# Three moves in the schedule of a fused adaLN block: the loads of stored attention results, the next q tile, and block 0's second norm

## The chip, the cores and the metric

The kernel runs on one core of one Trainium2 chip. Times are device microseconds of one execution (us). The metric is the median time of one launch; the trace is one profiled execution of the same program.

## The reference, cut to what matters

All arrays are fp32; S = 2048 tokens, D = 448, 16 heads of 28, F = 1792. Six vectors of the condition `c` (`sa`, `ca`, `ga` and `sb`, `cb`, `gb`) shift, scale and gate an attention branch and an MLP branch.

```python
mod = (_silu(c) @ w_mod).reshape(c.shape[0], 6, 1, -1)
sa, ca, ga, sb, cb, gb = (mod[:, 0], mod[:, 1], mod[:, 2], mod[:, 3], mod[:, 4], mod[:, 5])
h = _layernorm(x, axis=-1) * (1 + ca) + sa
x = x + ga * _A_ref(h, A_wqkv, A_wo)           # softmax attention over 16 heads, then @ wo
h = _layernorm(x, axis=-1) * (1 + cb) + sb
x = x + gb * _B_ref(h, B_w1, B_b1, B_w2, B_b2) # layernorm, @ w1 + b1, gelu, @ w2 + b2
```

So the second half begins with two layer norms in a row: the block's own, and after scale and shift the one inside `_B_ref`.

## The kernel before, in words

Matrix products keep fp32 accuracy by splitting operands into a high part `hi` and a rest `lo`, and adding three products. Tokens go in four blocks of 512 (`NB`), each of four tiles of 128.

**Phase 1** (to about 176 us) makes q, k and v. q and k are stored in DRAM (`dscr`) and read back in the layout that attention needs.

**Attention** is a loop over 16 units `u` = 0 to 15. Unit `u` is a group of four heads `g = u // 4` and a block of queries `qt = u % 4`. A unit has 16 steps, one per tile of 128 keys (`kt`), so the steps are numbered 0 to 255 and unit `u` begins at step 16u. One step emits, in this order:

1. at a fixed `kt`, `load_q(u + 1)`: two 256 KB loads of the next unit's q tile (L653 within `load_parts`);
2. `tick_late`, which puts ready row maxima into the q tile (L509 on VectorE, four small DMAs L512), once that tile was asked for;
3. twelve score matmuls into a two-bank PSUM tile `s` (L1162), with matmuls for the maxima of later units between them (L466) that VectorE reduces (L471), and two exponentials on ScalarE (L1167);
4. eight matmuls of the step before into `o` (L1132, function `av`); after a unit's last one `end_unit` copies `o` to `o_sb` on ScalarE (L1101);
5. whatever the table `sched` holds for this step. `at(step, fn)` appends to it; entries of one step run in the order in which they were appended. Entries made before the loop (norm, weights) thus stand ahead of those that `end_unit` makes within it.

Each engine runs its instructions in the order of emission, and so does SyncE's queue (SP), which issues nearly every DMA. An instruction that waits holds up all behind it on its engine.

**The end of a unit** is a chain of tasks counted from step `base + 1` with `base = 16(u + 1)`: `t_den` (the softmax sums go out by DMA, L880), `t_rec` (VectorE reciprocal L886, DMA to DRAM `drec` L888, broadcast back as `rb` L890), `t_split` (GpSimd multiplies `o_sb` by `rb`, L895) and `t_split2` (VectorE makes `hi`, L905; GpSimd makes `lo`, L906). Units 0 to 10 are "staged": they store hi and lo in DRAM (`doh`, L910). Units 11 to 14 finish a query block instead: `load_o` fetches the stored hi and lo of the earlier head groups into slots `a2h`, `a3h` and `b1h` (L868; four loads of 256 KB for unit 11, six for units 12 to 14), and the four tasks `t_wo(t)` at steps `base + 8` to `base + 11` multiply by `wo` (L386, nine to twelve matmuls into one PSUM tile), copy the result on ScalarE (L926) and add it to the residual `acc` on GpSimd (L927). Unit 15 needs no loads.

**PSUM tiles for small products** come from a ring, `ps_mx()`. During most of attention the ring has three banks. When no maxima are left, `third_tile(True)` gives two of them to a third score tile, and the ring is the single bank `m1`:

```python
    s_ring[:] = s_ring + ["s2"] if on else ["s1", "s0"]
    mx_ring[:] = ["m1"] if on else ["m1", "m2", "m2"]
```

**The second norm of block 0** (`ln2_stages(0)`) runs beside units 14 and 15. It has 14 numbered stages, one per step: the first statistics (stages 0 to 3, VectorE, L190 and L191; then GpSimd's power, L197), `mid` (4 to 7: VectorE normalises, L207; GpSimd multiplies and adds, L962 and L963), second statistics (6 to 9), `fin` (11 and 12: L207 and a copy, L968) and `addb` (10 to 13, GpSimd, L971). After them come four tasks `chunk(k)`, one per step: four transposes on TensorE (L267) into one `ps_mx()` tile, ScalarE's copy of it to `hi` (L994) and VectorE's subtraction for `lo` (L996, L998), both of which read that tile:

```python
            p = ps_o() if b and k == 3 else ps_mx()
            transposes(p, ys, k)
            hi = yT[b][0](k)
            act.copy(hi, p)
```

**Weights of the MLP** are fetched and split by `w_prep`: first loads at step 242 (L1014, L1016, L1017 and, for w2, L1035), then one item per step at steps 245 to 248 and 250 to 255 (VectorE, L1026 and L1027, or L1045 to L1048).

After step 255 comes the MLP (L1208 to L1237), which needs block 0's transposed norm at once.

The functions that the change touches, and their callers:

Of the kernel before, what the change touches and what calls it, by code (L numbers as in the profile page):

```python
# [27 lines left out]
NB = S // 512  # L28
NG = H // 4
NKT = S // 128  # L30
# [9 lines left out]
def tile_adaln_block(ctx: ExitStack, tc: tile.TileContext, x, wqkv, wo, w1, b1, w2, b2, c, w_mod, out):  # L40
# [29 lines left out]
    def nm(t):  # L70
        uid[0] += 1
        return f"{t}_{uid[0]}"

    def sbt(tag, shape, dt=F32, bufs=1):
        return sb.tile(shape, dt, tag=tag, name=nm(tag), bufs=bufs)

    def slot(tag, shape, dt=F32R):
        return sb.tile(shape, dt, tag="slot_" + tag, name=nm("slot_" + tag), bufs=1)
# [19 lines left out]
    def ps_mx():  # L98
        mx_ring.append(mx_ring.pop(0))
        return ps_tile(mx_ring[-1], 1 if mx_ring[-1] == "m1" else 2)  # L100

    def ps_o():
        return ps_tile("o")
# [4 lines left out]
    def f(t):  # L108
        return t.bitcast(F32)
# [254 lines left out]
    def put_spare(most=8):  # L364
        for kind, g, sl in spare[:most]:
            n = 4 * (4 * kind + g)
            for part in range(2):
                sp.dma_start(
                    by_head(f(dscr[1][part][3]))[:, n : n + 4, sl], by_head(f(dscr[kind][part][g]))[:, DH:32, sl],
                )  # L370
        del spare[:most]
# [10 lines left out]
    def mm_acc(p, terms, mid=None):  # L382
        for i, (a, b) in enumerate(terms):
            if mid and i == len(terms) // 2:
                mid()
            pe.matmul(p, a, b, start=(i == 0), stop=(i == len(terms) - 1))  # L386
# [223 lines left out]
    def finish_max(g, qt):  # L610
        while left[(g, qt)] > 0:
            emit_max(1)
# [35 lines left out]
    qst = {}  # L648
# [11 lines left out]
    def load_q(u):  # L660
        g, qt = divmod(u, NB)
        qst[u] = load_parts(f"b{u % 2}", 0, g, slice(qt * 512, (qt + 1) * 512))
# [33 lines left out]
    for b in range(NB):  # L696
        more = b + 1 < NB
        tasks = []
# [10 lines left out]
        for n, (tb, kind, g) in enumerate(tasks):  # L709
# [9 lines left out]
            k = n - (6, 4, 4, 4)[b]  # L719
# [17 lines left out]
            if more:  # L737
                k = n - (6, 4, 4, 4)[b]
# [122 lines left out]
    def last_g(qt):  # L861
        return NG - 2 if qt == NB - 1 else NG - 1

    def load_o(qt):
        for g, tag in zip(range(last_g(qt)), ("a2h", "a3h", "b1h")):
            t = slot(tag, [128, 2, 512])
            for part in range(2):
                sp.dma_start(f(t)[:, part, :], f(doh[part][g])[:, qt * 512 : (qt + 1) * 512])  # L868
            o_in[(qt, g)] = t

    def unit_end_tasks(u, o_sb):
        g, qt = divmod(u, NB)
        st = {}
        staged = g < last_g(qt)
        parts = [g] if g > last_g(qt) else list(range(g + 1))

        def t_den():
            q_ = pool if u == NU - 1 else sp
            den = sbt("den", [128, 16], bufs=2)
            q_.dma_start(den, o_sb[DH:128:32, :].rearrange("j (q r) -> j q r", r=16))  # L880
            st["den"] = den

        def t_rec():
            q_ = pool if u == NU - 1 else sp
            rec = st["den"]
            dve.reciprocal(rec, rec)  # L886
            drec = dr.tile([4, 512], F32, tag="drec", name=nm("drec"), bufs=2)
            q_.dma_start(drec.rearrange("j (q r) -> (j q) r", r=16), rec)  # L888
            rb = sbt("osb", [128, 512], bufs=2)
            q_.dma_start(rb, drec[:, None, :].broadcast_to([4, 32, 512]))  # L890
            st["rb"] = rb

        def t_split():
            st["on"] = st["rb"]
            pool.tensor_tensor(out=st["on"], in0=o_sb, in1=st["rb"], op=ALU.mult)  # L895

        def t_split2():
            on = st["on"]
            if u < NU - 1:
                hi = sbt("hi", [128, 512], F32R, bufs=3)  # L900
                lo = sbt("lo", [128, 512], F32R, bufs=3)
            else:
                hi = sb.tile([128, 512], F32R, tag=YTAGS[7], name="o_hi", bufs=1)
                lo = sbt("osb", [128, 512], F32R, bufs=2)
            dve.tensor_copy(hi, on)  # L905
            pool.tensor_tensor(out=lo, in0=on, in1=f(hi), op=ALU.subtract)  # L906
            st["hi"], st["lo"] = hi, lo
            if staged:
                for part in range(2):
                    sp.dma_start(f(doh[part][g])[:, qt * 512 : (qt + 1) * 512], f((hi, lo)[part]))  # L910

        def t_wo(t):
            def go():
                p = ps_mx()
                ts = slice(t * 128, (t + 1) * 128)
                terms = []
                for g_ in parts:
                    if g_ == g:
                        hi, lo = st["hi"][:, ts], st["lo"][:, ts]
                    else:  # L920
                        hi, lo = o_in[(qt, g_)][:, 0, ts], o_in[(qt, g_)][:, 1, ts]
                    w_hi, w_lo = wo_p[0][:, g_, :], wo_p[1][:, g_, :]
                    terms += [(hi, w_hi), (hi, w_lo), (lo, w_hi)]
                mm_acc(p[:, :D], terms)
                y = sbt("full", [128, 512], bufs=3)[:, :D]
                act.copy(y[:, :D], p[:, :D])  # L926
                pool.tensor_tensor(out=acc[qt][:, t, :], in0=acc[qt][:, t, :], in1=y[:, :D], op=ALU.add)  # L927

            return go


        times = (0, 4, 8, 9) if staged else (0, 1, 4, 5)
        tasks = list(zip(times, (t_den, t_rec, t_split, t_split2)))
        if len(parts) > 1 and not staged:
            tasks.append((0, lambda: load_o(qt)))
        if not staged:
            tasks += [(7 + t, t_wo(t)) for t in range(4)]
        return tasks
# [114 lines left out]
    NU = NG * NB  # L1053
    sched = {}

    def at(step, fn):
        sched.setdefault(step, []).append(fn)
# [10 lines left out]
    def b2_mul():  # L1068
        b2_row = sbt("row_b2g", [128, D])
        pool.tensor_tensor(out=b2_row, in0=rows["b2"][:, :D], in1=rows["gb"], op=ALU.mult)  # L1070
        rows["b2g"] = b2_row

    for i in range(5):
        at(1 + i, lambda: put_spare(1))
    for g in (1, 2):
# [3 lines left out]
    last0 = NKT * (NU - 1)  # L1079
    lnst = [ln2_stages(b) for b in range(NB)]  # L1080
    for i in range(14):
        at(last0 - 12 + i, lambda i=i: lnst[0][0](i))
    for k in range(NC):
        at(last0 + 3 + k, lambda k=k: lnst[0][1](k))
    q0, q1 = f"b{(NU - 2) % 2}", f"b{(NU - 1) % 2}"
    items = [w1_item(0, k, (q0, "a0")) for k in range(NC)]
    items += [w2_item(ft, ("v0", "a1")) for ft in range(0, 4)]
# [51 lines left out]
    for u in range(NU):  # L1139
        g, qt = divmod(u, NB)  # L1140
        for kt in range(NKT):
            step = u * NKT + kt
            if kt == 1 and u + 1 < NU and u + 1 not in qst:
                load_q(u + 1)
            if kt == NKT - 6 and u + 1 < NU:
                finish_max(*divmod(u + 1, NB))
            tick_late()
            if not (three or mxq or late):
                three = True
                third_tile(True)  # L1150
            pt = [slot(tags[step % len(tags)], [128, 2, 512], F32) for tags in ptags]
            n = n_maxima(step)
            n0 = 1 if n == 3 and step % 4 == 3 else 2

            ks, qs = kst[(g, kt // 4)], qst[u]
            kc = slice((kt % 4) * 128, (kt % 4 + 1) * 128)
            for hf in range(2):
                s2 = ps_s2()
                for term, (kp, qp) in enumerate(((0, 0), (1, 0), (0, 1))):
                    for jj in range(2):  # L1160
                        rows_ = slice(64 * hf + 32 * jj, 64 * hf + 32 * jj + DH + (term == 0))
                        pe.matmul(s2[:, jj, :], ks[rows_, kp, kc], qs[rows_, qp, :], start=(term == 0), stop=(term == 2))  # L1162
                    if hf == 0 and term < min(n0, n):
                        emit_max(1, 1)
                    if hf == 1 and term == 2 and n > n0:
                        emit_max(n - n0, 0)
                act.activation(pt[hf], s2, AF.Exp, scale=SCALE)  # L1167
            if step == 0:
                v_task(NB - 1, 3, ps_mx())
                emit_max(2)  # L1170
            if pend is not None:
                pu, pkt, pp, po = pend
                av(pu, pkt, pp, po)
                if pkt == NKT - 1:
                    end_unit(pu, po)
            if kt == 0:
                o = ps_o()
            pend = (u, kt, pt, o)
            if qt == NB - 1 and kt % 4 == 3 and g + 1 < NG:
                load_k(g + 1, kt // 4 if g else kt // 4 ^ 2)  # L1180
            for fn in sched.pop(step, ()):
                fn()
# [58 lines left out]
    for n in range(len(seq) + LAG):  # L1241
        if n < len(seq):
            b, i = seq[n]
# [53 lines left out]
```

## Time and profile before

| | |
|---|---|
| median of 3 runs | 1128.87 us (1128.83 to 1129.13) |
| the profiled execution's own time | 1130.08 us |
| its span (first to last instruction) | 1128.0 us |
| outside the span | 2.08 us |
| TensorE busy | 1116.4 us, 99% of the span |
| granted TensorE clock, mean | 1.00 |
| attention, by its `av` matmuls | 176.35 to 833.9 us |
| unit 13, 14, 15 from `t_den` to `t_den` | 692.2 to 742.0, to 789.6, to 834 us |

Reading it: PE is TensorE's matmuls, PEld its weight loads, DVE VectorE, ACT ScalarE, POOL GpSimd, SPq the DMA issues on SyncE's queue. In a timeline a row gives start and duration in us, engine, line of the kernel, operation, output and input tile, how many instructions were merged, and in square brackets how long the engine had been idle and what released it. In the chain of waits a row gives start, duration, and the work that nothing later could have started without. TensorE is pipelined, so busy TensorE is not TensorE at its peak, and a lost microsecond shows in the distance between equal steps better than in the busy share.

### The profile page before, as it was taken

Reading aid. Unit: us, or ns where it says so; the run is one execution under the profiler, and the core shown is the slowest. Engines: PE = TensorE matmul, PEld = TensorE weight load, DVE = VectorE, ACT = ScalarE, POOL = GpSimd, SP = SyncE. Lnnn points to the kernel's source line nnn. Section 1 sums busy time; section 2 is a strip of 40 time slices with the busy share of each in tenths; the row PEclk is TensorE's granted clock in tenths of the full one; section 3 lists DMA queues with packets and bytes.
Section 4 is the critical chain, followed back from the end, with each engine's and each line's share of the span. In section 5 each row is a group of like instructions: output and inputs, shape, how many; then the busy total and the mean of one; then the engine's idle time right before and its main releaser. Section 6 shows DMA issues by size and latency. Waiting matters only on the chain.

```text
span 1128.0 us, 20665 instructions
## 1 busy us (share of the span) xinstructions
PE 1116.4 (99%) x8319; PEld 670.1 (59%) x8319; DVE 843.7 (75%) x1485; ACT 672.0 (60%) x823; POOL 209.6 (19%) x211
## 2 busy tenths in 40 slices
PE   8999999999999999999999999999999999999998
PEld 6756674444444444444444454545468888888887
DVE  6968788999999999999999978595448853444322
ACT  4555657888887888788788867576752321111110
POOL 1533332110000000000000020217114504123000
PEclk9999999999999999999999999999999999999999
DMA  9562263121121211311111312020422100000000
GB/s 303 202 200 88 91 200 114 48 84 41 58 95 57 58 40 57 91 53 58 53 44 58 112 41 83 4 85 1 137 73 78 35 33 1 1 33 1 33 1 33
DMA packets 49341, 81.19 MB, mean 72 GB/s; under 512 B 12311, under 2 KB 18702, under 8 KB 49234
## 3 DMA queue, kind: packets, MB, share of 16 engines
q1 hardware_dynamic: 48762, 79.14, 22.1%
q8 instruction: 65, 1.06, 0.4%
q10 hardware_dynamic: 148, 0.46, 0.1%
q0 software_dynamic: 336, 0.28, 0.1%
q14 instruction: 30, 0.25, 0.1%
HBM read 55.04 MB, written 26.48 MB: 72 GB/s over the span
## 4 chain that ended last, share of the span: by engine, by line
PE 94%; DVE 3%; ACT 1%; DMA 1%; issue 1%; POOL 0%; SPq 0%; DVEq 0%; ACTq 0%; POOLq 0%
PE s L1162 26%; PE o L1132 22%; PE m L386 16%; PE pa L386 8%; PE m L466 6%; PE s L1232 3%; PE s L1233 3%; PE s L1231 3%; DVE mxp L471 2%; PE t L1232 1%; PE t L1233 1%; PE t L1231 1%; DMA slot_c<-in_w_mod_dram 1%; PE ma L466 1%; PE o L267 1%
## 5 line engine op out<-in xcount | busy, mean ns | idle before, releaser
L471 DVE TENSOR_REDUCE mxp<-m 128x1 f32<-128x512 f32 x884 | 568.8, 686 | 75.3 <-PE m L466 41.1
L1162 PE MATMUL s<-slot_b,slot_a 28*128 28x512 f32 (+1 forms) x3072 | 376.3, 420 | 0.0
L1162 PEld LDWEIGHTS s<-slot_b,slot_a 28*128 28x128 f32 (+1 forms) x3072 | 213.0, 184 | 247.4 <-ACT slot_c L1167 124.1
L466 PE MATMUL m<-kh,qh 28*128 28x512 f32 x863 | 287.6, 472 | 1.2 <-DVE mxp L471 0.9
L1167 ACT ACTIVATE slot_c<-s 128x1024 f32<-128x1024 f32 x170 | 174.3, 1025 | 75.9 <-PE s L1162 75.6
L1132 PE MATMUL o<-slot_c,v 128*32 128x512 f32 x680 | 178.8, 605 | 0.0
L1208 ACT ACTIVATE full<-m,b_col 128x512 f32<-128x512 f32 x56 | 38.6, 689 | 192.0 <-PE m L386 175.5
L1132 PE MATMUL o<-slot_c1h,v 128*32 128x512 f32 x512 | 134.7, 605 | 0.0
L1132 PE MATMUL o<-slot_c0h,v 128*32 128x512 f32 x512 | 134.7, 605 | 0.0
L1167 ACT ACTIVATE slot_c0h<-s 128x1024 f32<-128x1024 f32 x128 | 130.4, 1019 | 2.4 <-PE m L386 2.4
L1167 ACT ACTIVATE slot_c1h<-s 128x1024 f32<-128x1024 f32 x128 | 130.4, 1019 | 0.0
L1211 DVE CAST hi<-full 128x512 fp32r<-128x512 f32 x56 | 25.5, 455 | 134.6 <-ACT full L1208 134.6
L466 PEld LDWEIGHTS m<-kh,qh 28*128 28x128 f32 x863 | 114.3, 182 | 8.6 <-DVE mxp L471 5.1
L1167 ACT ACTIVATE slot_d<-s 128x1024 f32<-128x1024 f32 x86 | 88.1, 1025 | 39.3 <-PE s L1162 39.1
L895 POOL TENSOR_TENSOR osb<-osb,osb 128x512 f32<-128x512 f32 x16 | 20.9, 1307 | 441.1 <-DMA osb<-drec 356.8
L1132 PE MATMUL o<-slot_d,v 128*32 128x512 f32 x344 | 90.5, 605 | 0.4 <-ACT osb L1101 0.4
L386 PE MATMUL m<-y,slot_a 128*128 128x512 f32 x160 | 60.7, 395 | 0.0
L1132 PEld LDWEIGHTS o<-slot_c,v 128*32 128x32 f32 x680 | 24.5, 108 | 52.4 <-issue 49.5
L1212 DVE TENSOR_TENSOR lo<-full,hi 128x512 fp32r<-128x512 f32 x56 | 44.2, 788 | 5.9 <-DVE hi L1211 0.9
L471 DVE TENSOR_REDUCE mxp<-ma 128x1 f32<-128x512 f32 x54 | 35.6, 683 | 7.1 <-PE m L466 4.8
L386 PE MATMUL m<-y,slot_v 128*128 128x512 f32 x112 | 39.2, 396 | 0.0
L386 PE MATMUL m<-y,slot_b 128*128 128x512 f32 x112 | 39.0, 398 | 0.0
(316 smaller groups left out, 1626.7 us busy)
## 6 DMA issues: line engine op xcount, KB each, us to landing
slot_b<-d SPq DMA_DIRECT2D x32, 256.0 KB
slot_a<-d SPq DMA_DIRECT2D x32, 256.0 KB
d<-lo SPq DMA_DIRECT2D x28, 256.0 KB
d<-hi SPq DMA_DIRECT2D x16, 256.0 KB
osb<-drec SPq DMA_DIRECT2D x15, 256.0 KB
out_dram<-xn SPq DMA_DIRECT2D x16, 224.0 KB
raw<-in_B_w_dram SPq DMA_DIRECT2D x14, 224.0 KB
qh<-d SPq DMA_DIRECT2D x12, 256.0 KB
```

Of the source, the lines that this page charges most:

```text
L386: pe.matmul(p, a, b, start=(i == 0), stop=(i == len(terms) - 1))
L466: pe.matmul(m, qh_sb[(g, qt)][js, i * 128 : (i + 1) * 128], k[js, :], start=True, stop=True)
L471: dve.tensor_reduce(out=mxp[(g, qt)][:, i, j, cch : cch + 1], in_=m, op=ALU.max, axis=AX.X)
L1132: pe.matmul(o[32 * j : 32 * j + 32, :], v_sb[kt // 4][:, kt % 4, 4 * g + j, :], p[j // 2][:, j % 2, :], start=(kt == 0), stop=(kt == NKT - 1),
L1162: pe.matmul(s2[:, jj, :], ks[rows_, kp, kc], qs[rows_, qp, :], start=(term == 0), stop=(term == 2))
L1167: act.activation(pt[hf], s2, AF.Exp, scale=SCALE)
L1208: act.activation(gf, p, AF.Gelu_apprx_tanh, bias=b1_col[:, i : i + 1])
L1211: dve.tensor_copy(ghi, gf)
L1212: dve.tensor_tensor(out=glo, in0=gf, in1=f(ghi), op=ALU.subtract)
L1231: pe.matmul(pp, ghi[:, ts], w_hi, start=(m == 0), stop=False)
L1232: pe.matmul(pp, ghi[:, ts], w_lo, start=False, stop=False)
L1233: pe.matmul(pp, glo[:, ts], w_hi, start=False, stop=(m == NFT - 1))
```

## The change

Three things move; no instruction is added or removed.

- `load_o` for units 11 to 14 is no longer a task at `base + 1`, behind `t_den`. It stands in the table three steps before the end of the unit, at `base - 3`: steps 189, 205, 221 and 237.
- `load_q(u + 1)` is emitted at the unit's step 4 instead of its step 1.
- The second norm of block 0 is four steps later: its stages from steps 228 to 241 go to 232 to 245, its chunks from steps 243 to 246 go to 247 to 250.

```diff
         tasks = list(zip(times, (t_den, t_rec, t_split, t_split2)))
-        if len(parts) > 1 and not staged:
-            tasks.append((0, lambda: load_o(qt)))
         if not staged:
             tasks += [(7 + t, t_wo(t)) for t in range(4)]
...
+    for u in range(NU - NB - 1, NU - 1):
+        at(NKT * (u + 1) - 3, lambda qt=u % NB: load_o(qt))
...
     for i in range(14):
-        at(last0 - 12 + i, lambda i=i: lnst[0][0](i))
+        at(last0 - 8 + i, lambda i=i: lnst[0][0](i))
     for k in range(NC):
-        at(last0 + 3 + k, lambda k=k: lnst[0][1](k))
+        at(last0 + 7 + k, lambda k=k: lnst[0][1](k))
...
-            if kt == 1 and u + 1 < NU and u + 1 not in qst:
+            if kt == 4 and u + 1 < NU and u + 1 not in qst:
                 load_q(u + 1)
```

Here `last0` is 240, the first step of unit 15, `NKT` is 16, `NU` 16 and `NB` 4.

## The prediction

> **What bounds the kernel now.** I read the page first: busy time, then the chain of waits by engine.
>
> ```profile
> PE 1116.4 (99%) x8319; PEld 670.1 (59%) x8319; DVE 843.7 (75%) x1485; ACT 672.0 (60%) x823; POOL 209.6 (19%) x211
> PE 94%; DVE 3%; ACT 1%; DMA 1%; issue 1%; POOL 0%; SPq 0%; DVEq 0%; ACTq 0%; POOLq 0%
> ```
>
> TensorE carries 94% of the chain. An edit that moves other engines' work pays only where TensorE stands still for it. So I went through the chain of waits in order of time over units 13 to 15, where all three edits have their effects, and looked for steps longer than their like.
>
> ```profile
> 700.28 1.01 PE o L1132 x8
> ...
> 705.17 0.99 PE o L1132 x8
> ...
> 708.26 1.29 DVE mxp L471 x2
> ...
> 710.79 0.99 PE o L1132 x8
> ...
> 745.16 0.99 PE o L1132 x8
> ...
> 755.81 0.99 PE o L1132 x8
> ...
> 792.58 1.07 PE s L1162 x12
> ...
> 802.74 0.91 PE s L1162 x11
> ...
> 809.97 0.47 PE m L386
> 810.44 0.92 PE s L1162 x11
> ...
> 812.36 2.63 PE m L386 x12
> 814.99 0.91 PE s L1162 x12
> ...
> 824.07 0.91 PE s L1162 x12
> ...
> 829.96 1.07 PE s L1162 x12
> ```
>
> Three stalls show.
> - Unit 13: two steps with maxima take 4.89 us (700.28 to 705.17), the next two 5.62, with VectorE on the chain between. Lost: 0.73 us.
> - Unit 14, steps 228 to 231: four steps take 10.65 us (745.16 to 755.81) instead of 2 x 4.89. Lost: 0.87 us.
> - Unit 15: the score matmuls of steps 243, 247, 249, 250 and 252 begin at 792.58, 802.74, 810.44, 814.99 and 824.07. A plain step takes 1.96 us (824.07 to 829.96 is three), a step with a chunk 2.54 (four in 10.16), a `t_wo` step 4.55. Steps 247 and 248, one plain and one `t_wo`, take 7.70 instead of 6.51. Lost: 1.19 us, ahead of the last matmul of `t_wo(0)` at 809.97.
>
> Next, the timelines of VectorE, SP and GpSimd at these places tell why.
>
> ```profile
> 707.92 0.43 DVE L905 CAST hi<-osb 128x512 fp32r<-128x512 f32 x1 [1.12 <-POOL osb L895]
> ...
> 751.33 0.62 DVE L190 BATCH_NORM_STATS2 st<-acc 128x6 f32<-128x448 f32 x1
> 751.99 0.18 DVE L191 BATCH_NORM_AGGREGATE mv<-st 128x2 f32<-128x6 f32 x1
> ...
> 781.05 1.33 DVE L207 TENSOR_SCALAR xn<-xn,mv,rs 128x448 f32<-128x448 f32 x1 [2.13 <-POOL rs L197]
> ...
> 786.92 0.20 DVE L968 COPY xn<-xn 128x64 f32<-128x64 f32 x1
> 791.45 0.25 DVE L886 RECIPROCAL den<-den 128x16 f32<-128x16 f32 x1 [4.34 <-DMA den<-osb]
> ```
>
> ```profile
> 265.92 0.32 SPq L888 DMA_DIRECT2D drec<-den  x1
> 267.33 0.55 SPq L890 DMA_DIRECT2D osb<-drec  x1
> ...
> 737.58 0.80 SPq L653 DMA_DIRECT2D slot_b<-d  x2
> ...
> 768.65 2.28 SPq L512 DMA_DIRECT2D slot_b<-full  x4
> ...
> 790.25 0.89 SPq L868 DMA_DIRECT2D slot_a2h<-o  x2
> ...
> 793.30 0.90 SPq L1014 DMA_DIRECT2D raw<-in_B_w_dram  x2
> 794.30 0.50 SPq L888 DMA_DIRECT2D drec<-den  x1
> 800.32 0.56 SPq L890 DMA_DIRECT2D osb<-drec  x1
> ```
>
> ```profile
> 775.44 1.17 POOL L962 TENSOR_TENSOR xn<-xn,row_cb 128x448 f32<-128x448 f32 x1
> ...
> 778.90 1.14 POOL L927 TENSOR_TENSOR acc<-acc,full 128x448 f32<-128x448 f32 x1 [1.06 <-ACT full L926]
> 780.00 1.02 POOL L197 TENSOR_TENSOR rs<-ve,cst 128x4 f32<-128x4 f32 x1
> ...
> 806.71 1.28 POOL L895 TENSOR_TENSOR osb<-osb,osb 128x512 f32<-128x512 f32 x1 [20.95 <-ACT slot_c L1167]
> 808.60 1.32 POOL L906 TENSOR_TENSOR lo<-osb,hi 128x512 fp32r<-128x512 f32 x1 [0.60 <-DVE hi L905]
> ```
>
> In unit 13 VectorE stood 1.12 us at L905, waiting for the multiplication L895, with maxima queued behind. In unit 14 the first statistics (0.62 + 0.18 us, four times) sit between maxima that already fill VectorE. In unit 15 `lo` ends at 809.92, and TensorE goes on at 809.97. `lo` is late because `drec`, issued at 794.30 behind six loads of L868 and two weight loads, took until 800.32 to let `rb` go: 6.02 us, against 1.41 with nothing ahead (265.92 to 267.33). The page names an exponential as L895's releaser, but the row that fits is `rb`, issued 6.39 us before.
>
> **The change part by part.**
>
> **load_o, four steps earlier.** It leaves the queue between `den` and `drec`. At `base - 3` it waits for the last `t_wo` of the unit before, at `base - 5`. Behind it on SP stands only the next `den`, over 8 us later. Its data is wanted at `base + 8`. Price of the move: nothing. In unit 15 the two weight loads remain ahead of `drec`, now issued right behind `den`, and the reciprocal cannot come before 791.45. So `drec` goes at about 791.7, `rb` 1.41 to 6.02 us later. I take 2.5, near the quiet row, since a quarter of the load traffic is left: 794.2. With the old 6.39 us, L895 begins at 800.6 and `lo` is done near 804. At 6.02 it would be 807.5. `t_wo(0)` needs `lo` for its last product, after 809 in the new schedule (below), so even the upper end is covered. Gains: the 0.73 us of unit 13, where `rb` needs to be just over 1 us earlier, and the 1.19 us of unit 15. Each lies between 0 and its measured loss; I take all.
>
> **load_q, three steps later.** Before, it was issued well ahead of `den` (737.58 for unit 15). Now it comes behind `den`, and for units 11 to 13 behind `rb` too. The tile is written by the maxima DMAs only 31 us later (768.65) and read in the next unit. In staged units it also pushes L509 and the four maxima DMAs (2.28 us) from step 1 to step 4, ahead of `drec`. That costs `drec` at most these 2.28 us, while `t_split` is a fixed four steps (9.8 us) behind `t_rec` there. VectorE gets L509 beside the reciprocal, about half a microsecond together, less than one maximum. Cost: 0; if the cover were gone, the four maxima DMAs once per unit.
>
> **The second norm, stages.** The statistics go to steps 232 to 235. These are `t_wo` steps, in which almost no maxima are left, so VectorE is free. Gain: 0.87 us, bounds 0 and 0.87. The price is lateness. GpSimd's `mid` pairs (L962's 1.17 us and as much again for L963, some 2.4 us each) now follow the last residual addition, which ends at 780.04: four pairs to 789.7, statistics 0.8, power 1.02, so `fin` begins near 792. Before, the `fin` group took 6.07 us (781.05 to 787.12) beside `addb`, so it ends near 798. The first chunk's transposes would now come at about 802.3 (step 247 begins four plain steps after 792.5; scores and `av` take 1.9). Cover 4 us; cost 0.
>
> **The second norm, chunks: the term that decides.** They move from steps 243 to 246, where each shared its step with attention alone, to 247 to 250. Steps 248 to 251 are the `t_wo` steps of unit 14. The table's order puts the chunk first, then `t_wo`, and the ring is now the single bank `m1`. So `t_wo` must wait until ScalarE's copy and VectorE's subtraction have read the chunk out of it. Here is one chunk of before, all in one timeline.
>
> ```profile
> 797.67 0.99 PE L1162 MATMUL s<-slot_b,slot_a 29*128 29x512 f32 x12
> ...
> 800.50 0.59 ACT L994 CAST y<-m 128x512 fp32r<-128x512 f32 x1
> 801.12 0.69 DVE L996 TENSOR_TENSOR y<-m,y 128x512 fp32r<-128x512 f32 x1 [1.80 <-ACT y L994]
> ```
>
> The step's scores begin at 797.67 and the bank is free at 801.81, 4.14 us into the step. ScalarE reaches the copy only behind both exponentials. In the old place that time was hidden: after its transposes TensorE ran the next step's scores and `av`, which touch no ring bank. In the new place the twelve `t_wo` matmuls stand right behind. Add 0.05 for the hand-over (as `lo` to 809.97) and 2.63 for the twelve matmuls: a step with both takes 6.82 us instead of 4.55: 0.58 more for the chunk, and 1.69 in which TensorE waits.
>
> Old, step 243 to 252: 824.07 - 792.58 = 31.49. New: four plain steps 7.84, one chunk step 2.54, three double steps 20.46, one `t_wo` step 4.55, together 35.39. That is **+3.90**, with the 1.19 us already given back. Nothing behind this gains: the MLP starts when unit 15 ends, with the same queues.
>
> **Sum:** 3.90 - 0.73 - 0.87 = +2.30 us. The span goes from 1128.0 to 1130.3, the profiled execution from 1130.08 to 1132.4. The median shown lies 1.21 us under that execution, and I carry the difference over: 1128.87 + 2.3 = **1131.2 us**. If the two smaller gains come to nothing it is 1132.8. If plain steps also pack 0.08 us tighter and the bank frees 0.2 us sooner in each double step, 1130.3.
>
> **The rivals.**
>
> *Faster: the bank does not stop TensorE.* Place: between transposes and `t_wo` in steps 248 to 250. If that wait were zero, each double step would cost 4.55 + 0.58 = 5.13 instead of 6.82, the sum 2.30 - 5.07 = -2.8, the time 1126.1. It decides from a wait per step under some 0.9 us (2.3/3 less than 1.69). For it: none of the four old chunks stopped TensorE. Against it: they had 1.9 us of other matmuls behind them, and each next chunk did begin only after the subtraction. The Trainium skill ("PSUM — Partial Sum Buffer", section "PSUM bank collisions raise a hardware error") asks that accesses be guarded by bank and quadrant, so a reader and a writer of `m1` may not overlap; by that rule this rival has no room. No run shown here tests it. Chance 0.15. One double step of three without the wait would give 1129.5.
>
> *Slower still: VectorE is late for the subtractions.* Since step 245 it has a weight item per step ahead of them.
>
> ```profile
> 802.18 0.69 DVE L1027 TENSOR_TENSOR slot_a<-raw,slot_b 128x512 fp32r<-128x512 f32 x1
> ```
>
> With its cast an item is some 1.1 us, and it waits for a DMA. If each of three subtractions stands behind one, +3.3: 1134.5. Against it: in the new schedule weight loads start 3 us earlier and a double step leaves VectorE mostly idle. Chance 0.13.
>
> *The clock.* Stalls of 1.7 us in three steps running might lower TensorE's clock.
>
> ```profile
> 804.60:810.40 5.80, 5.01 (x40) 2.97 (x36) 3.20 (x6) 2.94 (x4) 2.61 (x2) 1.00 0.32 89
> ```
>
> The old stall sits in this stretch (columns: PE, PEld, DVE, ACT, POOL busy, then the clock), with 0.79 us of idle and a clock of 1.00. At half the clock the 15 us of matmuls in the double steps would take 15 more: 1146. The Trainium skill ("TensorE: Matmul & The Clock Gate", Part 1) has the clock halve after an idle window of about 3.4 us; by that rule gaps of half that length leave it alone, and the row agrees. Chance 0.02.
>
> *It does not do what it says:* `rb` is no earlier in unit 15 since the weight loads still precede it. This moves nothing, because `t_wo(0)` has itself moved behind the old 809.92. It lies within the forecast.
>
> **How the numbers follow.** Forecast 0.70, with its own range 1130.3 to 1132.8. A measurement of this kernel can tell about 0.2% from no change, 2.26 us, a line at 1131.1 that my forecast touches. I split its 0.70 into 0.40 over the line and 0.30 within. Slower: 0.40 + 0.13 + 0.02 = 0.55; same 0.30; faster 0.15. The range leaves out the free bank (0.15) and the clock (0.02) but takes in one wait saved and late subtractions: 1129.5 to 1134.5.
>
> **What would show it.** TensorE waiting for L996 before L386 in steps 248 to 250, about 1.7 us each, and score-to-score distances near 6.8 there; chunk-free steps 243 to 246 at 1.96; no wait for L906; `rb` within 3 us of `drec`; no idle at L905 in unit 13; no 0.87 us loss in unit 14. It is wrong if double steps are near 5.1, or if L905 or the first chunk is what they wait for.

## The result and the profile after

The changed kernel takes 1132.65 us (median of nine runs, 1132.11 to 1133.04) against 1128.87 for the kernel before in the same nine rounds (1127.58 to 1132.12). The ratio is 1.0031, 95% interval 1.0021 to 1.0040: slower by about 3.5 us. The forecast was 1131.2, slower, within 1129.5 to 1134.5.

In the changed file lines 936 to 1072 of the kernel before stand two lines higher: the chunk's copy is L992, its subtractions L994 and L996, `mid` L960 and L961, the weight loads from L1012. Below, the kernels without the early `load_o` (later norm alone, later next q alone) keep the numbers of before; there L996 and L998 are the subtractions. First the page of the changed kernel: span, busy times, chain by engine.

```profile
span 1130.1 us, 20669 instructions
...
PE 1115.2 (99%) x8319; PEld 669.3 (59%) x8319; DVE 840.8 (74%) x1485; ACT 672.1 (59%) x823; POOL 209.2 (19%) x211
...
PE 93%; DVE 3%; DMA 1%; ACT 1%; issue 1%; SPq 0%; POOL 0%; DVEq 0%; ACTq 0%; POOLq 0%
```

The page hardly differs; the change is in a few steps. The chain of waits of the changed kernel in order of time, units 13, 14 and 15 (start, duration, work):

```profile
704.86 0.99 PE o L1132 x8
...
709.75 0.99 PE o L1132 x8
...
744.14 0.99 PE o L1132 x8
...
753.92 0.99 PE o L1132 x8
...
790.65 1.06 PE s L1162 x11
...
798.62 1.05 PE s L1162 x11
...
801.27 0.92 PE s L1162 x12
...
803.14 1.02 ACT slot_c0h L1167
804.15 0.49 ACT y L992
...
804.66 0.70 DVE y L994
...
805.41 2.71 PE m L386 x12
808.12 0.92 PE s L1162 x10
...
814.97 0.92 PE s L1162 x12
...
821.80 0.91 PE s L1162 x11
...
826.34 0.91 PE s L1162 x12
```

- Unit 13: the two steps that took 5.62 us now take 4.89. Unit 14: steps 228 to 231 take 9.78 instead of 10.65. Both stalls are gone.
- Unit 15: steps 243 to 246 take 7.97 together, 247 takes 2.65, and the double steps 248 to 250 take 6.85, 6.85 and 6.83. From step 243 to 252 it is 35.69 us instead of 31.49.
- Inside a double step the chain leaves TensorE: exponential, copy out of `m1`, subtraction, and only then `t_wo`.

All waits of TensorE's matmuls in units 11 to 15 (total, times, longest):

```profile
PE m L386 <- DVE y L994: 3.3, 2, 1.6
PE m L386 <- DVE y L996: 1.6, 1, 1.6
...
```

Three waits of 1.6 us for the subtraction (L994, and L996 for the last chunk), and none for L906 any more.

### The profile page after: what moved, and what is told of

Same layout as the page of the kernel before. It is cut to its first block, busy times and chain, and to the rows that moved or that the text cites. A ratio compares the mean times of both kernels' runs of the same rounds, so it can differ in the third digit from the quotient of the medians.

```text
span 1130.1 us, 20669 instructions
## 1 busy us (share of the span) xinstructions
PE 1115.2 (99%) x8319; PEld 669.3 (59%) x8319; DVE 840.8 (74%) x1485; ACT 672.1 (59%) x823; POOL 209.2 (19%) x211
## 4 chain that ended last, share of the span: by engine, by line
PE 93%; DVE 3%; DMA 1%; ACT 1%; issue 1%; SPq 0%; POOL 0%; DVEq 0%; ACTq 0%; POOLq 0%
PE s L1162 26%; PE o L1132 22%; PE m L386 16%; PE pa L386 8%; PE m L466 6%; PE s L1232 3%; PE s L1233 3%; PE s L1231 3%; DVE mxp L471 2%; PE t L1232 1%; PE t L1233 1%; PE t L1231 1%; DMA slot_c<-in_w_mod_dram 1%; PE o L267 1%; PE ma L466 1%
## 5 line engine op out<-in xcount | busy, mean ns | idle before, releaser
L895 POOL TENSOR_TENSOR osb<-osb,osb 128x512 f32<-128x512 f32 x16 | 21.0, 1310 | 430.0 <-DMA osb<-drec 367.1
```

## The experiments

All ratios are against the kernel before, timed in the same job. The nine-run result is the changed kernel's; "+" and "-" in us are the ratio times 1128.5.

| kernel | ratio, 95% interval | us |
|---|---|---|
| changed, again | 1.0032 (1.0020 to 1.0045) | +3.6 |
| early load_o alone | 0.9993 (0.9985 to 1.0002) | -0.8 |
| later norm alone | 1.0091 (1.0077 to 1.0105) | +10.3 |
| later next q alone | 1.0023 (1.0012 to 1.0033) | +2.6 |
| changed, chunk behind `t_wo` | 1.0001 (0.9992 to 1.0010) | +0.1 |
| changed, four double steps | 1.0050 (1.0038 to 1.0063) | +5.6 |
| changed, chunks in steps 252 to 255 | 0.9979 (0.9971 to 0.9988) | -2.4 |
| changed, norm packed | 0.9982 (0.9972 to 0.9991) | -2.0 |
| packed, next q in step 1 | 0.9984 (0.9975 to 0.9993) | -1.8 |
| changed, next q in step 1 | 1.0033 (1.0020 to 1.0045) | +3.7 |

The three parts alone add up to +12.1, together they make +3.6. So two things had to be found out: whether the double steps are the cost, and how the parts protect each other.

### The changed kernel again, and the kernel before in a second profile

> The changed kernel once more, beside the parts below. By its trace: +3.8 us in unit 15 for three double steps, with the old 1.2 us stall given back inside that, -0.7 in unit 13, -0.9 in unit 14, so about +2.2 us (ratio 1.002). The median of its nine runs stood 3.8 us above the kernel before (1.0033). If the 1.5 us between these belong to the change, 1.003 comes again; if they are scatter of the kernel before, the ratio falls to about 1.002.

> The kernel before, once more, for a second profile. Its profiled execution took 1130.08 us where its median is 1128.5 to 1128.9, and the changed kernel stands 3.6 us above it by medians but 2.2 by the two traces. Theory: the waits for rb (0.73 us in unit 13, 1.19 in unit 15) hang on how fast transfers land and differ between executions; an execution near the median shows one or both of them smaller. Rival: the difference lies ahead of attention (the first av at 176.35 us) or is spread evenly.

The first came again at 1.0032, so the 3.6 us belong to the change. The second (one profiled execution, no edit) took 1128.2 us with a span of 1126.1: 0.7 us below the median of the main measurement, where the first profile was 1.2 above it. Here are its waits of TensorE's matmuls in units 11 to 15, then SP and GpSimd around `rb` in unit 15:

```profile
...
PE m L466 <- DVE mxp L471: 0.4, 1, 0.4
```

```profile
793.53 0.38 SPq L888 DMA_DIRECT2D drec<-den  x1
798.92 0.56 SPq L890 DMA_DIRECT2D osb<-drec  x1
...
804.62 1.28 POOL L895 TENSOR_TENSOR osb<-osb,osb 128x512 f32<-128x512 f32 x1 [19.62 <-DMA osb<-drec]
```

The wait for `lo` is missing from the list. `drec` took 5.39 us and `rb` 5.70, against 6.02 and 6.39 in the execution on which the prediction rested. Step for step against that execution, unit 13 is 0.38 us shorter and step 248 is 1.09 us shorter. So those stalls vary between executions. The kernel with the later norm alone (below) also has the old loads in unit 13, and its unit 13 is 0.35 us shorter than in the first profile too; of these three executions, the one behind the prediction has the longest stall. Between this execution and the changed kernel's the spans differ by 4.0 us. The scatter ahead of attention (0.56 us between the two profiles of the kernel before) is part of what remains.

### The bank: chunk behind t_wo, four double steps, none

The first of these turns the order round inside steps 247 to 250, by entering the chunk after `end_unit` has entered `t_wo`:

```diff
-        at(last0 + 7 + k, lambda k=k: lnst[0][1](k))
+        at(last0 + 2, lambda k=k: at(last0 + 7 + k, lambda: lnst[0][1](k)))
```

> The changed kernel with one thing turned round: in steps 247 to 250 the chunk stands behind t_wo, not ahead of it. Theory, the bank m1 is what costs: the chunk's transposes now wait only for the residual's copy (L926, about 0.7 us after t_wo's last matmul), and the chunk's own readers are hidden behind the next step's scores, so a double step takes about 5.9 us instead of 6.85: 2.8 us less than the changed kernel, about +0.8 against before. Rival, the double steps are long because of the work in them and not of the wait: same as the changed kernel, +3.6.

Measured +0.1, or 3.5 us less than the changed kernel; the expected +0.8 lies in the interval. The chain of waits in one of its double steps and the list of waits say how:

```profile
806.12 0.54 ACT full L926
...
806.70 0.65 PE m L267 x4
807.36 0.91 PE s L1162 x11
...
813.18 0.92 PE s L1162 x10
```

```profile
PE m L267 <- ACT full L926: 1.9, 3, 0.7
```

The same work in the same steps now takes 5.82 us (807.36 to 813.18), with 0.65 of waiting instead of 1.64. It is the wait, not the work.

Next, one more chunk in a `t_wo` step (`last0 + 8 + k`, steps 248 to 251):

> The changed kernel with the chunks one step later still, 248 to 251, so that all four share a step with t_wo. Theory, each shared step costs 6.85 where a t_wo step takes 4.55 and a chunk alone adds 0.55: one more shared step is 1.7 us more than the changed kernel, about +5.3 against before. Rival, the stall has a fixed part paid once: less than 1 us more.

+5.6, 2.0 us over the changed kernel where 1.7 was expected, with an interval on each of about 1.4. The waits count it exactly:

```profile
PE m L386 <- DVE y L994: 4.9, 3, 1.6
PE m L386 <- DVE y L996: 1.6, 1, 1.6
```

Four waits of 1.6 us, no fixed part. And no double step (`last0 + 12 + k`, steps 252 to 255):

> The changed kernel with the four chunks in steps 252 to 255, where no t_wo stands. Theory, a chunk costs 0.55 us alone and 2.3 us beside t_wo: three double steps of 6.85 become t_wo steps of 4.55 and chunk steps of 2.5, about 5.1 us less than the changed kernel, -1.5 us against before (ratio 0.9987). Rival: the MLP's first matmuls then wait for the last chunk, and some 1 to 2 us come back at the end of unit 15.

-2.4, some 5 to 6 us under the changed kernel. The rival had a little in it: at the end of unit 15 the chain runs through the last chunk.

```profile
829.57 0.60 ACT y L992
...
830.20 0.71 DVE y L996
...
830.95 7.92 PE m L386 x33
```

The MLP's first matmuls start behind that subtraction, but the matmuls waited only 0.2 us for it in all.

### load_o alone

```diff
-        if len(parts) > 1 and not staged:
-            tasks.append((0, lambda: load_o(qt)))
...
+    for u in range(NU - NB - 1, NU - 1):
+        at(NKT * (u + 1) - 3, lambda qt=u % NB: load_o(qt))
```

> The early load_o alone, norm and next q as before. Theory: the six loads stood ahead of drec, so rb comes earlier; the wait at L905 in unit 13 (0.73 us) and the wait of t_wo(0) for lo in unit 15 (1.19 us) go, the statistics in unit 14 stay: -1.9 us, ratio 0.9983. Rival, nothing on the path depends on rb: 0.

-0.8, with an interval that touches 0, where -1.9 was expected. SP in unit 13:

```profile
696.03 0.31 SPq L888 DMA_DIRECT2D drec<-den  x1
697.47 0.55 SPq L890 DMA_DIRECT2D osb<-drec  x1
```

`drec` takes 1.44 us, the quiet value, where it took 4.62 in the profile of before. Neither of the two waits is in its trace any more, so the mechanism holds. What is missing is the size: the kernel before does not lose the whole 1.9 us in every execution. In its second profile the two places lose 0.35 and 0.10 us. The statistics of unit 14, which this kernel leaves where they were, still make that unit as long as before.

### The norm alone

```diff
-        at(last0 - 12 + i, lambda i=i: lnst[0][0](i))
+        at(last0 - 8 + i, lambda i=i: lnst[0][0](i))
-        at(last0 + 3 + k, lambda k=k: lnst[0][1](k))
+        at(last0 + 7 + k, lambda k=k: lnst[0][1](k))
```

> The second norm four steps later alone, loads as before. Theory for the collision alone: three double steps of 6.8 us, minus the statistics (0.87 us), and the late lo mostly covered: +3.0 to +3.6 us. But the early load_o may protect more than lo: VectorE makes hi (L905, emitted in step 246) ahead of the first chunk's subtraction (step 247). If rb is late as before, L905 waits until about 807, the subtraction behind it until 808, and the second chunk's transposes, due at about 804, wait for the bank: some 4 us more, +7 in all, ratio 1.006. Rival, the load and the norm do not touch each other: the sum of the parts, +3.0.

+10.3: above even the higher of the two. Its chain of waits in unit 15:

```profile
792.80 5.90 DMA drec<-den
...
798.76 6.63 DMA osb<-drec
...
805.52 1.27 POOL osb L895
...
806.81 0.43 DVE hi L905
807.24 0.60 DVE y L996
807.84 1.11 DVE slot_b L1026
...
810.41 4.85 PE m L386 x12
```

As expected, `drec` and `rb` are as slow as before, VectorE stands 6.60 us at L905, the first chunk's subtraction waits behind it, and so the bank is not free for the second chunk: TensorE's transposes waited 4.25 us. The part that was not expected is in the next view of the same kernel: the stretch and its length, busy time of PE, PEld, DVE, ACT and POOL, then the granted clock:

```profile
803.64:805.50 1.86, 0.00 (x1) 0.00 (x0) 0.00 (x0) 0.97 (x2) 0.00 (x0) 1.00 0.55 114
805.50:815.74 10.24, 6.44 (x20) 5.08 (x24) 4.53 (x7) 1.03 (x2) 2.53 (x2) 0.50 0.19 53
```

The clock stood at half for 10.24 us. The twelve `t_wo` matmuls took 4.85 us instead of 2.7, the four transposes 1.11 instead of 0.59: some 2.7 us, which with the expected 7 makes about 9.7. It is not this execution alone: the mean granted clock of all four executions is 0.995 to 0.997. So the early `load_o` is worth 0.8 us by itself and about 7 under the later norm.

### The next q alone, and put back

```diff
-            if kt == 1 and u + 1 < NU and u + 1 not in qst:
+            if kt == 4 and u + 1 < NU and u + 1 not in qst:
```

> The next q tile in step 4 alone. Theory: its landing has over 20 us of cover in the last units, and in staged units the maxima's DMAs ahead of drec are covered by the four steps between reciprocal and multiplication: 0, within 0.3 us. Rival, den no longer behind the maxima's DMAs or drec now behind them matters: a difference in steps of units 2 to 11.

+2.6, not 0. Its profiled execution was the slowest of its eight (1134.26 against a median of 1131.43), so the size of a stall there is an upper one. SP, GpSimd and VectorE in unit 13:

```profile
701.16 0.55 SPq L890 DMA_DIRECT2D osb<-drec  x1
701.80 0.90 SPq L653 DMA_DIRECT2D slot_b<-d  x2
...
707.82 1.26 POOL L895 TENSOR_TENSOR osb<-osb,osb 128x512 f32<-128x512 f32 x1 [27.45 <-ACT slot_c L1167]
...
709.12 0.43 DVE L905 CAST hi<-osb 128x512 fp32r<-128x512 f32 x1 [2.78 <-POOL m L501]
```

`load_q` now goes out right behind `rb`, and from the issue of `rb` to L895 it is 6.66 us; in the kernel before, with `load_q` far ahead, 5.03 (701.56 to 706.59). The changed kernel, where `load_q` also follows `rb`, has 6.14 (698.07 to 704.21), and 4.90 (697.74 to 702.64) with the next q put back. So a transfer beside `rb` costs it over a microsecond. VectorE stands 2.78 us at L905 instead of 1.12 and the maxima behind it come late. (L501, the releaser named, is a small memset that GpSimd runs right behind L895; L905 reads what L895 wrote.)

The wait is not all. Unit 13 takes 4.80 us more than in the first profile of before, and the longest wait of a matmul is 1.9 us. Behind that wait the granted clock stood at half for 6.83 us (last section), which by itself costs about 3.4 us, an estimate from half of that time. Two of the eight executions, at a mean granted clock of 1.00, still took 1131.58 and 1131.83 us, so a lower clock is not the only cost; how the 2.6 divides is open. Within the whole change, with only this line put back to `kt == 1`, it is different:

> The changed kernel with only the next q put back to step 1. Theory: inside the whole change the late q costs nothing, since the early load_o has taken the wait for rb off the path: same as the changed kernel, +3.6 against before. Rival: it costs there what it cost alone (ratio 1.0023), then +1.

1.0033 against 1.0032: nothing. There `rb` goes out some 3 us earlier, and L905 finds its input ready in either case.

### A version faster than both

Against the changed kernel; the second of the two also has `load_q` back in step 1:

```diff
-        at(last0 - 8 + i, lambda i=i: lnst[0][0](i))
+        at(last0 + (i // 2 - 8 if i < 4 else i - 10), lambda i=i: lnst[0][0](i))
-        at(last0 + 7 + k, lambda k=k: lnst[0][1](k))
+        at(last0 + 3 + k, lambda k=k: lnst[0][1](k))
```

> The changed kernel with the norm packed: the four statistics two a step in steps 232 and 233 (t_wo steps with few maxima), every later stage in steps 234 to 243, the chunks back in 243 to 246. Theory: early load_o and free statistics keep their gains, no double step: as the chunks after the t_wo steps, 5.1 us less than the changed kernel, -1.5 us against before (0.9987). Rival: GpSimd's norm work among the residual additions makes fin late for the first chunk, and TensorE waits there.

> The packed norm and the early load_o, with the next q back in step 1, so its loads no longer run behind rb. Theory: rb lands about 1.2 us sooner after its issue (4.9 instead of 6.1 us), but with the loads of stored results gone from before it nothing waits for it any more: same as packed, 0.998 of before. Rival: the margin still counts in some executions, then up to 0.5 us less.

0.9982 and 0.9984, medians 1127.12 and 1126.94 beside 1129.19 and 1128.8 for the kernel before in the same jobs: by about 2 us faster than the kernel before, and not to be told apart from one another or from the chunks in steps 252 to 255 (1127.08). In both, TensorE's matmuls wait once in units 11 to 15, 0.4 us for the copy of `o` in unit 15, as in every version. So the rival of a late `fin` is not seen.

## Why the prediction was right

**The bank `m1`, the deciding term: right, in place and size.** 6.82 us a double step was forecast, 6.83 to 6.85 came; a wait of 1.69, and 1.64 came; 35.39 us for steps 243 to 252, and 35.69 came. Turning the order round, adding a fourth shared step and taking all away moved the time as the wait says. The faster rival, that the bank does not stop TensorE, is excluded.

**load_o: right in the mechanism, its gains oversized.** `drec` follows the weight loads, and `rb` left 2.8 us after it (2.5 forecast). SP and GpSimd of the changed kernel:

```profile
789.89 0.33 SPq L888 DMA_DIRECT2D drec<-den  x1
792.72 0.55 SPq L890 DMA_DIRECT2D osb<-drec  x1
...
798.04 1.29 POOL L895 TENSOR_TENSOR osb<-osb,osb 128x512 f32<-128x512 f32 x1 [3.60 <-DMA osb<-drec]
799.93 1.28 POOL L906 TENSOR_TENSOR lo<-osb,hi 128x512 fp32r<-128x512 f32 x1 [0.60 <-DVE hi L905]
```

`lo` was done at 801.2, before the 804 forecast. Most of that is unit 15 beginning 1.9 us earlier (its first `av` row stands at 787.67, before at 789.61); the rest is mainly `rb`, which took 5.3 us and not the 6.39 carried over. The rival that `rb` comes no earlier in unit 15 is excluded (792.72 against 800.32).

As a difference of two profiled executions the sum was close: +2.30 forecast, 1132.24 - 1130.08 = +2.16 measured. The medians lie 3.78 apart (3.5 by the ratio), because the profile of before stood 1.21 us above its median and that of the changed kernel 0.41 below. So the step that was off is "I carry the difference over": it took a difference of one execution to be the same in every kernel. The two terms 0.73 and 1.19 hang on the same execution. In the second one the stalls were 0.38 and 1.09 smaller, and with those the same sum is 3.90 + 1.09 - 0.35 - 0.87 = 3.8. That this meets the 3.78 of the medians so closely is luck: the second execution stood 0.7 us below the median, and steps 243 to 252 took 0.30 more than forecast. But it shows where the forecast of 2.3 fell short: it credited stalls that are not always there.

**The statistics: right.** 0.87 us was forecast and came (steps 228 to 231 in 9.78 instead of 10.65).

**The norm's lateness: right that it is covered.** The first chunk's transposes were not held up (step 247 took 2.65 us). What the prediction did not say is that this cover hangs on the early `load_o`: without it L905 stands in front of the chunk's subtraction.

**The rival of a late VectorE: wrong.** In the double steps (rows of the first two) VectorE stood idle until the copy was done:

```profile
804.66 0.69 DVE L994 TENSOR_TENSOR y<-m,y 128x512 fp32r<-128x512 f32 x1 [0.91 <-ACT y L992]
...
811.51 0.69 DVE L994 TENSOR_TENSOR y<-m,y 128x512 fp32r<-128x512 f32 x1 [5.10 <-ACT y L992]
```

**load_q: 0 in the whole change, for another reason than given.** The prediction asked when its own data is wanted, and priced a lost cover at four small DMAs per unit. What it costs is the transfer that it runs beside: `rb`, 1.6 us slower in that execution. When nothing else is changed the time rises by 2.6 us; in the one trace of that, the lower clock has a part in it.

**The clock: right for this change, but with less margin than it said.** Three waits of 1.64 us, each with 5.2 us of matmuls around it, left it alone (first of the three below). The waits of 1.86 and 1.89 us in the last section were followed by half the clock, so "gaps of half that length" are not safe in general.

```profile
801.20:808.05 6.85, 5.21 (x37) 3.27 (x36) 3.43 (x6) 3.19 (x5) 0.01 (x1) 1.00 0.21 51
```

## What to carry to other kernels

When work moves into another step, ask which buffer it shares there and who must finish with it: the engine's total is the same, but a single bank passed between two users in one step exposes both readers, and the order of the two decides how much. Price a DMA that is moved by what it now flies beside, not only by when its data is wanted. Before a stall that hangs on a transfer is credited as a gain, look at a second execution, and price parts together where one engine's queue holds both.

## What was not expected of the hardware

The granted clock fell to half after less than 2 us without matmuls. In the kernel with the later norm alone TensorE stood from 803.64 to 807.89, and the clock fell at 805.50, 1.86 us into that wait (rows in its section). In the kernel with the later q alone the wait was 1.89 us, from 708.31 to 710.20, and the clock fell at 710.97:

```profile
708.31:710.97 2.66, 0.68 (x8) 0.36 (x9) 1.85 (x4) 0.28 (x1) 2.09 (x3) 1.00 0.01 4
710.97:717.80 6.83, 6.83 (x27) 4.07 (x28) 2.35 (x5) 2.05 (x2) 0.00 (x0) 0.50 0.01 1
```

The Trainium skill ("TensorE: Matmul & The Clock Gate", Part 1) has the clock halve after an idle window of about 3.4 us. Neither trace agrees with that as an unbroken wait: in both the clock fell after less than 2 us without matmuls. The two stretches at half the clock lasted 10.24 and 6.83 us, three and two times 3.41. Three waits of 1.64 us with 5.2 us of matmuls between them did nothing.

What the bound is stays open. It cannot be the wait alone: in the profile of the kernel with the chunks in steps 252 to 255 the clock stood at half from 175.44 to 178.85, at the start of attention, though TensorE was busy for 3.13 of the 3.44 us before. In no other trace here did it fall there.
